# A quarter of the weights' low parts: one VectorE step in place of two GpSimd steps, with new instruction sequences

## The chip, the cores and the metric

The kernel runs on one core of a Trainium2 chip. The metric is device time in microseconds (us); before the change it is 901.27 us, the median of 3 runs (898.79 to 902.77). Five engines work side by side, each through its own list of instructions in order: TensorE (PE, with PEld for its weight loads), VectorE (DVE), ScalarE (ACT), GpSimd (POOL) and SyncE (SP), which issues the DMAs. An instruction that waits holds up everything behind it on its own engine.

## What is computed

Clustered attention over 4 batches, 8 heads, 768 positions of 64 elements, and on its output an MLP with a rational activation:

```python
mask = q_assign[:, :, :, None] == k_assign[:, :, None, :]      # nearest of 16 centroids, by cosine
scores = np.where(mask, scale * q @ k.T, -1e9)
x = softmax(scores) @ v                                        # -> (3072, 512)
h = x @ w_in                                                   # 512 -> 2048
P = a[0] + a[1] * h + a[2] * h * h + a[3] * h * h * h
Q = 1.0 + abs(b[0]) * abs(h) + abs(b[1]) * h * h
out = (P / (Q + 1e-6)) @ w_out                                 # 2048 -> 512
```

The results are wanted more exactly than one product of 16-bit numbers gives. So the kernel splits each matrix into a high part in f16 and a low part, the rest, also in f16, and adds three products: high by high, high by low, low by high.

## The kernel before

The program is made in two passes. The functions `weights`, `v_scale`, `g_scale`, `prep`, `attend`, `attend_keys` and `moe` only note down operations: engine, a cost in ns, what is read and written, which buffers are claimed. Each operation has a number, in the order in which it was noted. Then `Plan.order` emits them; the order on each engine is not planned in this kernel but given, as the lists of numbers in `ORDER` (lines 31 to 174). So a change in the number of operations renumbers what follows, and the lists must be written anew.

`weights(name, i, vt)` prepares one of 8 blocks of the MLP's weights, 4 of `w_in` ("wi") and 4 of `w_out` ("wo"), in the order wi0, wo0, wi1, wo1 and so on. A block has four chunks `c` of 128 partitions by 512 words. For each chunk:

- SP loads the raw 64-bit words (tile `rwi` or `rwo`).
- ACT takes the magnitude (line 672), and DVE makes an f32 number of it in three instructions: a shift (685), an or with the low word (690) and the sign (697). The tile is then `wwi` or `wwo`.

When all four are there, PE sums the squares (711), a power-of-two scale comes out of it, and for each pair of chunks `m`:

- ACT writes the high part into `win` or `wout`, 1024 columns at a time (749; in the trace all ACT work is on line 535, in the helper).
- For each of the two chunks POOL scales the f32 number in place (line 766) and subtracts the high part from it (line 773), which leaves the low part in f16.

The code has held another way for that last step since before: where `share("wlo", c)` is true, one DVE instruction does scale and subtract (lines 755 to 762). `share(name, i)` reads a fraction from `K`; `wlo` is not in `K`, so it is 0 and no chunk takes that way.

The blocks are spread over the first 200 us or so, between the work of batch 0. In that batch `attend_keys` works on four pairs of heads: `s` scores by PE (1391), the largest of each row by DVE out of PSUM (`top`, 1418), the scores turned round (`z`, 1470), the exponent by ACT (`at`), and the product with the values in f32 (1489, 1495). From about 180 us on `moe` (first product `ph`, 1622; second product `po`, 1733) runs on one batch, while `prep` and `attend` (scores 1261, 1277, 1323, values 1343) work on the next one. Since all engines serve both, the lists of `ORDER` set which goes first.

The names that the prediction uses: `win`, `wout` the split weights; `top`, `s`, `z`, `at`, `px`, `rs` of the attention; `ph`, `po`, `t`, `u` of the MLP; `tk`, `tq` the scaled keys and queries (1060, with a copy in 1080).

Of the kernel before, what the change touches and what calls it, by code (L numbers as in the profile page):

```python
# [27 lines left out]
K = {'ghd': 0.0, 'rvp': 0, 'look': 62.89, 'mulp': 0.4, 'sub': 0, 'xn': 14, 'NR': 8, 'sgp': 1, 'scp': 1, 'vsc': 0.75, 'sup0': 0, 'stk': 2, 'lop': 0, 'mgp': 0, 'rvn': 2, 'tq2': 2, 'at': 3, 'es': 4, 'vn': 3, 'ah': 5, 'rel': 0, 'twin': 1, 'pet': '_01', 'avs': 3, 'ksum': 1, 'fst': '_0', 'hpa': 1}  # L28
# [36 lines left out]
""",  # L65
    "DVE": """
# [310 lines left out]
def clustered_attention_moe_kernel(  # L377
# [167 lines left out]
    def dve(ns, fn, r, w, vt, claim=(), chain=None, lock=False, behind=()):  # L545
        return op("DVE", ns, fn, r, w, vt, claim, chain=chain, lock=lock, behind=behind)
# [1307 lines left out]
```

## Time and profile before

| | |
|---|---|
| time, median of 3 runs | 901.27 us (898.79 to 902.77) |
| the profiled execution | 901.28 us |
| its span (first to last instruction) | 899.1 us |
| PE, DVE, ACT, POOL busy | 851.8, 800.4, 772.2, 595.9 us |
| mean granted clock of TensorE | 0.994 |

Busy times are sums over the span; an engine may be busy and yet not be what the others wait for. In the timelines a bracket at a line's end tells how long the engine stood idle before that instruction and what ended the wait. The columns of a table of stretches are: the stretch, its length, the busy time of each engine in it with the number of its instructions, the granted clock, the share of the DMA engines and GB/s.

### The profile page before, as it was taken

Reading aid. Unit: us, or ns where it says so; the run is one execution under the profiler, and the core shown is the slowest. Engines: PE = TensorE matmul, PEld = TensorE weight load, DVE = VectorE, ACT = ScalarE, POOL = GpSimd, SP = SyncE. Lnnn points to the kernel's source line nnn. Section 1 sums busy time; section 2 is a strip of 40 time slices with the busy share of each in tenths; the row PEclk is TensorE's granted clock in tenths of the full one; section 3 lists DMA queues with packets and bytes.
Section 4 is the critical chain, followed back from the end, with each engine's and each line's share of the span. In section 5 each row is a group of like instructions: output and inputs, shape, how many; then the busy total and the mean of one; then the engine's idle time right before and its main releaser. Section 6 shows DMA issues by size and latency. Waiting matters only on the chain. (4 is left out here: it accounts for less than half of the span.)

```text
span 899.1 us, 20440 instructions
## 1 busy us (share of the span) xinstructions
PE 851.8 (95%) x7781; PEld 589.0 (66%) x7781; DVE 800.4 (89%) x1603; ACT 772.2 (86%) x1194; POOL 595.9 (66%) x623
## 2 busy tenths in 40 slices
PE   3799999898999999899999999999999999999997
PEld 2467676675767676566676666676667666667663
DVE  7998989689999999999999999999989989777775
ACT  7568787899999999998999999999998989767664
POOL 1354775599887978676888878788887866222221
PEclk9999999999999999999999999999999999999999
DMA  8488574658989688999799898888568855300000
GB/s 269 129 227 179 157 213 125 187 99 184 168 182 208 128 162 179 171 174 210 145 192 167 150 204 173 163 155 160 113 130 147 153 109 104 83 2 24 1 24 24
DMA packets 344802, 129.82 MB, mean 144 GB/s; under 512 B 322560, under 2 KB 338944, under 8 KB 344704
## 3 DMA queue, kind: packets, MB, share of 16 engines
q1 hardware_dynamic: 344704, 128.52, 67.4%
q8 instruction: 61, 1.00, 0.5%
q14 instruction: 37, 0.30, 0.1%
HBM read 41.98 MB, written 6.29 MB: 54 GB/s over the span
## 5 line engine op out<-in xcount | busy, mean ns | idle before, releaser
L1733 PE MATMUL po<-wout,u 128*128 128x512 f16 x1152 | 266.5, 379 | 0.1
L1622 PE MATMUL ph<-x,win 128*128 128x256 f16 x2304 | 264.6, 273 | 0.8 <-DVE t L1648 0.7
L1622 PEld LDWEIGHTS <-win 128*128 128x128 f16 x2304 | 225.2, 98 | 39.6 <-issue 1.1
L1662 POOL TENSOR_TENSOR s<-s,u 128x512 f32<-128x512 f32 x96 | 124.0, 1311 | 102.3 <-ACT s L535 54.9
L1733 PEld LDWEIGHTS <-u 128*128 128x128 f16 x1152 | 111.6, 98 | 120.1 <-issue 2.0
L1323 DVE SCALAR_TENSOR_TENSOR ah<-s,su,ah 128x768 f16<-128x768 f32 x144 | 143.2, 1012 | 13.1 <-ACT ah L535 11.5
L1277 DVE TENSOR_SCALAR_CACHE_REDUCE s<-s,cc 128x768 f32<-128x768 f32 x144 | 143.6, 1019 | 8.2 <-PE s L1261 7.1
L535 ACT ACTIVATE s<-s,nm 128x768 f32<-128x768 f32 x144 | 126.1, 877 | 12.1 <-DVE s L1277 10.0
L535 ACT ACTIVATE ah<-s,su 128x768 f16<-128x768 f32 x144 | 127.3, 904 | 5.3 <-ACT s L535 3.2
L1261 PE MATMUL s<-sk,sq 128*128 128x384 f16 x576 | 113.2, 329 | 6.3 <-DVE ah L1323 5.8
L1722 POOL TENSOR_TENSOR u<-s,u 128x512 f16<-128x512 f32 x72 | 83.5, 1169 | 50.5 <-DVE s L1715 26.8
L1685 POOL TENSOR_TENSOR s<-s,u 128x512 f32<-128x512 f32 x72 | 100.3, 1404 | 19.1 <-ACT u L535 18.7
L1261 PEld LDWEIGHTS <-sq 128*128 128x128 f16 x576 | 52.8, 98 | 49.9 <-DVE ah L1323 11.6
L1343 PE MATMUL px<-at,vhi 128*64 128x256 f16 x864 | 74.7, 275 | 2.5 <-DMA at<-ah 1.7
L1643 DVE TENSOR_TENSOR t<-ph,t 128x512 f32<-128x512 f32 x96 | 65.2, 683 | 8.1 <-ACT t L535 7.8
L535 ACT ACTIVATE u<-ph 128x512 f32<-128x512 f32 x96 | 57.3, 598 | 17.1 <-PE ph L1622 16.3
L1343 PE MATMUL px<-at,vlo 128*64 128x256 f16 x432 | 60.8, 273 | 0.0
L1715 DVE SCALAR_TENSOR_TENSOR s<-s,t 128x1024 f32<-128x1024 f32 (+1 forms) x49 | 60.2, 1228 | 0.5
L535 ACT ACTIVATE u<-t 128x1024 f16<-128x1024 f32 (+1 forms) x49 | 51.1, 1043 | 8.8 <-DVE s L1678 4.5
L1343 PEld LDWEIGHTS <-vhi 128*64 128x64 f16 x864 | 46.9, 110 | 17.0 <-issue 8.1
L535 ACT ACTIVATE t<-ph,gk 128x512 f32<-128x512 f32 x72 | 55.7, 778 | 0.0
L535 ACT ACTIVATE at<-z,cc 128x768 f32<-128x768 f32 x48 | 42.0, 897 | 15.7 <-PE z L1470 14.8
(222 smaller groups left out, 1541.6 us busy)
## 6 DMA issues: line engine op xcount, KB each, us to landing
rwi<-in_moe_w_in_dram SPq DMA_DIRECT2D x16, 512.0 KB, 4.8
rwo<-in_moe_w_out_dram SPq DMA_DIRECT2D x16, 512.0 KB, 4.6
rk<-in_k_dram SPq DMA_DIRECT2D x32, 192.0 KB, 3.2
rq<-in_q_dram SPq DMA_DIRECT2D x32, 192.0 KB, 3.3
rvm<-in_v_dram SPq DMA_DIRECT2D x16, 384.0 KB, 4.4
rv<-in_v_dram SPq DMA_DIRECT2D x16, 384.0 KB, 4.1
out_dram<-ob SPq DMA_DIRECT2D x11, 512.0 KB, 3.0
at<-ah SPq DMA_TRANSPOSE x144, 3.9
```

What stands on the lines that cost most here:

```text
L535: lambda: nc.scalar.activation(out=out(), in_=in_(), func=func, **{a: (x() if callable(x) else x) for a, x in kw.items()}),
L1261: nc.tensor.matmul(sc.ap[:, i, :SH], lhsT=st["q" + x].ap[:, j, t, :], rhs=st["k" + x].ap[:, j, ks, :].rearrange("p t c -> p (t c)"), start ...
L1277: lambda nm=nm, view=view: ts(out=view(), in0=view(), scalar1=cc.ap, scalar2=None, op0=ALU.mult, op1=ALU.min, accum_out=nm.ap),
L1323: lambda part=part, view=view, su=su: stt(out=part(1), in0=view(), scalar=su.ap, in1=part(0), op0=ALU.mult, op1=ALU.subtract),
L1343: nc.tensor.matmul(px.ap[j * D : (j + 1) * D, :], lhsT=vv.ap[:, j, kt, :], rhs=at[j].ap[:, p_, kt].rearrange("p t c -> p (t c)"), start=(i ...
L1622: nc.tensor.matmul(ph[i].ap[:, fi * TW : (fi + 1) * TW], lhsT=win[f // 4][:, wpart, c, f % 4 * P : (f % 4 + 1) * P], rhs=xs[c].ap[:, xpart ...
L1643: lambda i=i, th=th, ph=ph: tt(out=th[i].ap, in0=ph[i].ap, in1=th[i].ap, op=ALU.mult),
L1662: lambda i=i, sh=sh, uh=uh: nc.gpsimd.tensor_tensor(out=sh[i].ap, in0=sh[i].ap, in1=uh[i].ap, op=ALU.mult),
L1685: lambda i=i, sh=sh, uh=uh: nc.gpsimd.tensor_tensor(out=sh[i].ap, in0=sh[i].ap, in1=uh[i].ap, op=ALU.mult),
L1715: lambda tw=tw, sw=sw: stt(out=sw(), in0=sw(), scalar=2.0, in1=tw(), op0=ALU.subtract, op1=ALU.mult),
L1722: lambda i=i, sh=sh, gl=gl, g16=g16, e=(nc.vector if gld else nc.gpsimd): e.tensor_tensor(out=gl[i].ap, in0=sh[i].ap, in1=g16()[:, 0, i * ...
L1733: nc.tensor.matmul(po[ti].ap, lhsT=g16()[:, part, c0 : c0 + P], rhs=wout[f // 4][:, wpart, f % 4], start=(k == 0 and f == f_first), stop=( ...
```

## The change

`K` gets `'wlo': 0.25`. With it `share("wlo", c)` is true for c = 3 alone, so in each of the 8 blocks the fourth chunk's low part is made by one DVE instruction, and the two POOL instructions for it are gone. Each block has 35 operations in place of 36.

The lists in `ORDER` are written anew for all five engines, over the whole run. With the numbers brought back to the old ones, the longest run of operations that stands in the same relative order in both lists is 1094 of 1381 on DVE, 858 of 1001 on ACT, 662 of 789 on PE, 405 of 588 on POOL and 234 of 348 on SP. Most moves are by one to four places.

A further branch, `share("sgm", c)`, is added in the loop over the chunks, but `sgm` is not in `K`: it is never taken.

```diff
-K = {'ghd': 0.0, ..., 'hpa': 1}
+K = {'ghd': 0.0, ..., 'hpa': 1, 'wlo': 0.25}

 ORDER = {   (all five lists)
...
-            dve(
-                dc(512),
-                lambda w=w, word=word: stt(
-                    out=w.ap, in0=word(1), scalar=-2147483648, in1=w.ap, op0=ALU.bitwise_and, op1=ALU.bitwise_or
-                ),
-                [raw], [w], vt, [*hold, tok], lock=True,
-            )
+            if share("sgm", c):
+                act(
...
+            else:
+                dve(
+                    dc(512),
+                    lambda w=w, word=word: stt(
+                        out=w.ap, in0=word(1), scalar=-2147483648, in1=w.ap, op0=ALU.bitwise_and, op1=ALU.bitwise_or
+                    ),
+                    [raw], [w], vt, [*hold, tok], lock=True,
+                )
```

The step that is taken for c = 3, unchanged in the code:

```python
dve(
    dc(512, 1),
    lambda c=c, h=hl[d]: stt(
        out=h.ap[:, 1], in0=wf(c), scalar=sc(), in1=h.ap[:, 0], op0=ALU.mult, op1=ALU.subtract
    ),
    [ws[c], ws_], [hl[d]], vt, [wp[m], ptok[m]], lock=True,
)
```

## Rows read from the trace of the kernel before

**Rows 1.** The page's first part: busy time, share of the span, instructions.
```profile
PE 851.8 (95%) x7781; PEld 589.0 (66%) x7781; DVE 800.4 (89%) x1603; ACT 772.2 (86%) x1194; POOL 595.9 (66%) x623
```

**Rows 2.** Table of stretches, the run in three parts.
```profile
0.00:28.00 28.00, 12.54 (x136) 10.58 (x137) 21.25 (x73) 20.32 (x35) 4.39 (x21) 1.00 0.78 260
28.00:215.00 187.00, 168.91 (x1989) 123.21 (x1988) 166.14 (x352) 145.10 (x246) 122.46 (x154) 0.97 0.65 164
215.00:894.00 679.00, 670.30 (x5656) 455.20 (x5656) 612.40 (x1180) 606.09 (x915) 469.08 (x449) 1.00 0.69 134
```

**Rows 3.** Table of stretches, the part in which weights are prepared, by stage.
```profile
28.00:62.00 34.00, 26.82 (x262) 17.05 (x262) 33.80 (x62) 17.67 (x28) 18.14 (x24) 0.95 0.64 168
62.00:90.00 28.00, 27.95 (x361) 21.32 (x358) 24.23 (x59) 23.59 (x39) 12.34 (x18) 1.00 0.76 184
90.00:110.00 20.00, 19.10 (x221) 13.60 (x221) 19.70 (x36) 13.79 (x24) 14.22 (x16) 1.00 0.46 147
...
130.00:153.00 23.00, 21.25 (x214) 14.89 (x214) 22.75 (x47) 13.98 (x26) 13.51 (x20) 1.00 0.43 128
153.00:180.00 27.00, 23.54 (x344) 18.19 (x341) 18.12 (x44) 23.68 (x44) 16.91 (x26) 0.94 0.74 195
180.00:215.00 35.00, 30.25 (x312) 23.17 (x311) 31.33 (x69) 34.03 (x59) 31.82 (x35) 0.95 0.65 131
```

**Rows 4.** Lines 766 and 773: ns min/median/max, first and last start in us.
```profile
L766 POOL TENSOR_SCALAR wwi<-wwi,wis x16: 687/693/1911, 34.5 to 175.4; 128x512 f32<-128x512 f32 x16
...
L773 POOL TENSOR_TENSOR win<-wwi,win x16: 1148/1158/1866, 36.7 to 186.5; 128x512 f16<-128x512 f32 x16
```

**Rows 5.** DVE's timeline: start, duration, line, operation, tiles.
```profile
25.14 0.69 DVE L690 SCALAR_TENSOR_TENSOR wwi<-rwi,wwi 128x512 int32<-128x512 int32 x1
25.75 0.69 DVE L690 SCALAR_TENSOR_TENSOR wwo<-rwo,wwo 128x512 int32<-128x512 int32 x1
```

**Rows 6.** Groups on DVE, 28 to 215 us: busy us, mean ns, idle before.
```profile
L697 DVE SCALAR_TENSOR_TENSOR wwo<-rwo,wwo 128x512 int32<-128x512 int32 x15 | 12.1, 807 | 0.1
...
L1060 DVE SCALAR_TENSOR_TENSOR tq<-rq,qsc,tq 128x768 f16<-128x768 f32 x5 | 6.8, 1357 | 0.5 <-ACT tq L535 0.5
...
L1060 DVE SCALAR_TENSOR_TENSOR tk<-rk,ksc,tk 128x768 f16<-128x768 f32 x5 | 5.2, 1045 | 0.0
```

**Rows 7.** Timelines around 85 us: ACT's high part for wi1, and DVE.
```profile
84.26 1.14 ACT L535 ACTIVATE win<-wwi,wis 128x1024 f16<-128x1024 f32 x1
...
85.71 0.48 DVE L1540 SCALAR_TENSOR_TENSOR rs<-px,ev,rs 128x256 f32<-128x256 f32 x1 [0.60 <-ACT rs L535]
```

**Rows 8.** Timelines around 380 us, of DVE (two lines) and of PE.
```profile
379.95 0.35 DVE L1080 COPY tk<-tk 128x768 f16<-128x768 f16 x1
380.22 1.01 DVE L1323 SCALAR_TENSOR_TENSOR ah<-s,su,ah 128x768 f16<-128x768 f32 x1
...
381.29 0.82 PE L1261 MATMUL s<-sk,sq 128*128 128x384 f16 x4 [0.89 <-DVE ah L1323]
```

**Rows 9.** Timelines: POOL's last low part, and PE's first use of `wout`.
```profile
196.24 1.45 POOL L773 TENSOR_TENSOR wout<-wwo,wout 128x512 f16<-128x512 f32 x1
...
215.72 1.46 PE L1733 MATMUL po<-wout,u 128*128 128x512 f16 x6
```

**Rows 10.** PE's timeline, three waits between 158 and 207 us.
```profile
160.76 1.86 PE L1470 MATMUL z<-sq,sk 128*128 128x256 f16 x12 [2.44 <-ACT at L535]
...
204.75 0.71 PE L1532 MATMUL px<-rs,pick 128*128 128x128 f32 x4 [2.77 <-DVE rs L1524]
...
206.88 2.74 PE L1261 MATMUL s<-sk,sq 128*128 128x384 f16 x8 [1.30 <-DVE ah L1323]
```

**Rows 11.** ACT's timeline just before the first of these waits ends.
```profile
159.25 0.66 ACT L535 ACTIVATE wwo<-rwo 128x512 f32<-128x512 f32 x1 [1.80 <-DMA rwo<-in_moe_w_out_dram]
```

**Rows 12.** Table of stretches, two of 10 us with a lower granted clock.
```profile
160.00:170.00 10.00, 9.24 (x116) 7.40 (x115) 7.59 (x16) 9.93 (x18) 4.04 (x9) 0.83 0.88 256
200.00:210.00 10.00, 5.93 (x46) 3.19 (x35) 9.23 (x21) 9.94 (x18) 9.63 (x9) 0.83 0.94 198
```

More of the change, by code (lines that the diff above doesn't have):

```diff
@@ L25 @@
 M_BIG, M_MID, M_LOW = 2.0 ** 15, 2.0 ** 7, 2.0 ** -4
-K = {'ghd': 0.0, 'rvp': 0, 'look': 62.89, 'mulp': 0.4, 'sub': 0, 'xn': 14, 'NR': 8, 'sgp': 1, 'scp': 1, 'vsc': 0.75, 'sup0': 0, 'stk': 2, 'lop': 0, 'mgp': 0, 'rvn': 2, 'tq2': 2, 'at': 3, 'es': 4, 'vn': 3, 'ah': 5, 'rel': 0, 'twin': 1, 'pet': '_01', 'avs': 3, 'ksum': 1, 'fst': '_0', 'hpa': 1}
+K = {'ghd': 0.0, 'rvp': 0, 'look': 62.89, 'mulp': 0.4, 'sub': 0, 'xn': 14, 'NR': 8, 'sgp': 1, 'scp': 1, 'vsc': 0.75, 'sup0': 0, 'stk': 2, 'lop': 0, 'mgp': 0, 'rvn': 2, 'tq2': 2, 'at': 3, 'es': 4, 'vn': 3, 'ah': 5, 'rel': 0, 'twin': 1, 'pet': '_01', 'avs': 3, 'ksum': 1, 'fst': '_0', 'hpa': 1, 'wlo': 0.25}
 ORDER = {
     "ACT": """
[32 rows of a table removed]
[32 rows of a table added]
 """,
     "DVE": """
[44 rows of a table removed]
[44 rows of a table added]
 """,
     "PE": """
[25 rows of a table removed]
[25 rows of a table added]
 """,
     "POOL": """
[19 rows of a table removed]
[19 rows of a table added]
 """,
     "SP": """
[12 rows of a table removed]
[12 rows of a table added]
 """,
@@ L694, in weights @@
             )
-            dve(
-                dc(512),
-                lambda w=w, word=word: stt(
-                    out=w.ap, in0=word(1), scalar=-2147483648, in1=w.ap, op0=ALU.bitwise_and, op1=ALU.bitwise_or
-                ),
-                [raw], [w], vt, [*hold, tok], lock=True,
-            )
+            if share("sgm", c):
+                act(
+                    ac(512) + 65, lambda word=word: word(1).bitcast(F32), lambda word=word: word(1).bitcast(F32), AF.Sign, [raw], [raw],
+                    vt, [tok],
+                )
+                op(
+                    "POOL", 1400,
+                    lambda w=w, word=word: nc.gpsimd.tensor_tensor(
+                        out=w.ap.bitcast(F32), in0=w.ap.bitcast(F32), in1=word(1).bitcast(F32), op=ALU.mult
+                    ),
+                    [raw], [w], vt, [*hold, tok],
+                )
+            else:
[3 more added lines that the diff above has]
+                        out=w.ap, in0=word(1), scalar=-2147483648, in1=w.ap, op0=ALU.bitwise_and, op1=ALU.bitwise_or
+                    ),
+                    [raw], [w], vt, [*hold, tok], lock=True,
+                )
         gram = misc([P, P], F32, f"{name}g{i}")
```

264 rows, old and new, of the table ORDER are left out of this document.

## The prediction

> **What bounds the kernel now.** I read the page's first part, then tables of stretches, then timelines at the places where TensorE (PE) stands still. PE is busy for 851.8 of 899.1 us [rows 1], so the whole span holds 47 us in which it does nothing. The table in three parts says where: 15.5 us of them before 28 us (28 less 12.54), 18.1 between 28 and 215 us, 8.7 between 215 and 894 us, and the last 5 us, when the output leaves [rows 2]. The weights are prepared in the first two parts. After 215 us PE is 98.7% busy: what reaches that point late ends late by the same amount, and little can be won behind it except out of those 8.7 us.
>
> By stage, the part from 28 to 215 us has different limits [rows 3]. From 28 to 62 us VectorE (DVE) is busy 33.80 of 34 us and PE only 26.82: there DVE sets the pace. From 62 to 90 us PE is full (27.95 of 28) and DVE has 3.8 us to spare. From 90 to 110 and from 130 to 153 us both are nearly full (DVE 19.70 of 20 and 22.75 of 23, PE 19.10 and 21.25). From 153 to 180 us no engine is full: the stage is made of waits on each other. From 180 to 215 us ACT is the fullest, 34.03 of 35. GpSimd (POOL) is nowhere near full before the last stage. So the change takes work from an engine that is mostly not a limit and gives it to one that is a limit, alone or with PE, in three of these stages.
>
> **The change, part by part.** The profiled execution took 901.28 us, its span 899.1 and 2.2 around it; the median of the runs shown is 901.27, so a sum made against the profiled execution needs no correction.
>
> Removed: 8 times one scaling at 0.69 us and one subtraction at 1.16 us on POOL [rows 4], 14.8 us of work. That time itself is worth nothing at first: nobody waits for the low parts. The last of them is done at 197.7 us (196.24 and 1.45), and the first product with `wout` comes at 215.72 [rows 9].
>
> Added: 8 instructions on DVE, each of two inputs in SBUF and 512 columns. The trace shows no such instruction with this line. The nearest rows are of line 690, the same operation on 512 columns: 0.69 us for one, and two in a row start 0.61 us apart (25.14 and 25.75), so that is what one takes from DVE [rows 5]. To it comes what such an instruction loses when POOL works beside it: the 15 of line 697 on `wwo` have a mean of 0.807 us, 0.12 above the undisturbed 0.69 [rows 5, 6]. So one costs 0.73 us, and all eight 5.8 us of DVE.
>
> It also waits, like POOL's step before, for ACT's high part, and behind it on DVE stand row maxima (line 1418), for which PE's scores wait. The tightest place is the third: ACT writes that high part until 85.40 us (84.26 and 1.14), and the new list puts the instruction behind line 1540, which started at 85.71 [rows 7]. So the wait is over in time as long as both engines run as before, and I cost it at nothing; if ACT came 1 us later there, DVE would lose up to that 1 us, in a stage where it has 3.8 to spare.
>
> How much of this lies on the path? The new list of DVE in the diff tells next to which operations each one stands: the first in the stage from 28 to 62 us, the second and third between 62 and 90, the fourth between 90 and 110, the fifth and sixth between 130 and 153, the last two between 180 and 215. The first is on the path in full, 0.73. The second and third are covered by a full PE, the last two by DVE's 3.7 us of idle time in their stage [rows 3]; without that cover they would cost 0.73 each. The fourth to the sixth stand where DVE and PE are both nearly full; PE stands still for only 0.90 and 1.75 us there, so most of the delay is hidden, and I charge a third, 3 × 0.73 / 3 = 0.73. Together +1.5 us; the ends are 0 and 5.8.
>
> Given back: POOL's instructions disturb those of DVE less. Line 697 on `wwo` lost 15 × 0.12 = 1.8 us, line 1060 on `tq` 5 × (1.357 − 1.045) = 1.6 us against its twin on `tk` [rows 6], 3.4 us in all. A quarter of the 64 low-part instructions goes, so a quarter of that, −0.9 us. It can't be below nothing by much (the ends are 0 and −3.4).
>
> On the shared ports the rule of the Trainium skill ("SBUF — State Buffer", section "Who interferes with whom") is sharper than these means: a VectorE instruction with two SBUF inputs and a GpSimd instruction that reads SBUF exclude each other for the whole instruction, and who issues first wins. By that rule the new instruction pays nothing or up to a whole POOL instruction, not 0.12 us each time. In the rows only the mean over 15 is seen, and it speaks for few meetings; what the many would cost is the slower rival below.
>
> Moved: all five lists. Where an instruction of no urgency stood ahead of one that PE waits for, a new order can win that instruction's time. One such place can be read out of the diff: the copy of line 1080 at 379.95 us stands ahead of line 1323 at 380.22, for which PE waits 0.89 us [rows 8], and in the new list it comes later; that is worth 0.27 us, −0.3. I could not find one that loses for certain: on SP several transposes and loads go back behind others that wait for their data, but their users come much later. The rest of the moves I put at 0, between −8.7 us (all of PE's idle time after 215 us [rows 2]) and the same amount the other way, both unlikely.
>
> Sum: 1.5 − 0.9 − 0.3 = +0.3 on 901.28, that is **901.5 us**.
>
> **The rivals.** *Faster, by the stalls between 158 and 210 us.* PE waits there 2.44, 2.77 and 1.30 us [rows 10], and in two stretches of 10 us the granted clock falls to a mean of 0.83, a part of each at 1.2 in place of 2.4 GHz, after PE had stood still for some of the time [rows 12]; a loss of (1 − 0.83) × 10 = 1.7 us each at most. Together that is 6.5 + 3.4 = 9.9 us. These waits end with ACT and DVE, which have POOL's work in their chains; the last stage is the one in which POOL is busiest, 31.82 of 35 us [rows 3], and four of the removed instructions are near it. If half of the 9.9 us goes, and another 1 us of waits after 215 us with it, the time is 901.5 − 5.0 − 1.0 = 895.5. For it: the moves are many and go through all lists, and the stalls are few and large. Against it: the first wait ends only when ACT, held up for 1.80 us by a DMA of `rwo`, goes on [rows 11], and SP's list is the same around that DMA; DVE's work ahead of the other two is nearly the same set of instructions in both lists.
>
> *Slower, by the ports.* The new instruction stands on DVE near the other low parts of its block, which POOL still makes. If it meets a subtraction at its start, it waits up to the whole 1.16 us [rows 4], and everything behind it on DVE, row maxima and scores, waits too, and PE for those. The four that stand where DVE is nearly full would then cost 4 × (0.61 + 1.16) = 7.1 us in place of 1.5: 901.5 + 5.6 = 907.1. It decides from a mean wait of about 0.6 us for each of the four (4 × 1.21 − 1.5 = 3.4 us more, and with the relief gone 4.6). Against it: the mean loss of the same kind of instruction is 0.12 us [rows 5, 6].
>
> *Nothing but noise:* the change does what it says (`share` gives one chunk of four), but PE's full stages cover it and the moves cancel. That is 901.3, within the forecast's own range.
>
> **How the numbers follow.** A measurement of this kernel can tell about 0.5% from no change, 4.5 us. The forecast, with the third case in it, has 0.46 (897 to 905.8, from the ends of its terms); faster by the stalls or by the moves, 0.31; slower by the ports, or by a move that costs, 0.23. For 8 times in 10 the range must reach well into both rivals: from 894 us, the faster rival with 1.5 us more, to 908 us, the slower one with 1 us more.
>
> **What would show it.** Right: 16 instructions of lines 766 and 773 fewer in all, eight of line 758 on DVE with a mean near 0.8 us; DVE's busy time from 28 to 215 us up by 3 to 5 us; PE's start of the first `po` within 2 us of 215.7; PE's idle time after 215 us between 7 and 11 us. Wrong: the first `po` over 3 us earlier or later; the stretch from 200 to 210 us without its fall of the clock (the faster rival), or line 758 with a mean over 1.2 us (the slower one); or an idle time of PE after 215 us that has changed by more than 3 us, which no term of the sum foresees.

## The result: 0.6% slower, and the profile after

Beside each other the changed kernel took 905.68 us (median of 16 runs, 901.53 to 909.85), the kernel before 900.90 (median of 16, 898.04 to 903.17). The ratio is 1.0059, 95% interval 1.0046 to 1.0071: 5.3 us slower by the ratio, 4.1 to 6.4. The forecast was 901.5; the time lies in the stated range, on its slower side, nearer to the rival by the ports (907.1) than to the forecast. The profiled execution took 908.59 us, 2.9 above the median, and that will matter below.

From line 697 on the lines of the changed kernel stand 13 later (697 is 710, 1060 is 1073, 1733 is 1746); the new step is on line 771, POOL's pair on 779 and 786. First the page's first part, as in [rows 1]:

```profile
PE 855.2 (94%) x7781; PEld 591.5 (65%) x7781; DVE 805.3 (89%) x1611; ACT 775.1 (85%) x1194; POOL 585.2 (65%) x607
```

The table of stretches, as in [rows 2, 3, 12]:

```profile
0.00:28.00 28.00, 11.18 (x115) 9.56 (x116) 21.00 (x73) 19.46 (x34) 5.51 (x21) 1.00 0.82 258
28.00:215.00 187.00, 166.85 (x1964) 121.64 (x1963) 166.23 (x349) 141.34 (x236) 106.05 (x135) 0.98 0.63 160
215.00:901.60 686.60, 677.09 (x5707) 460.31 (x5705) 617.35 (x1190) 613.65 (x925) 473.69 (x452) 1.00 0.69 134
...
28.00:62.00 34.00, 26.66 (x257) 17.77 (x256) 30.98 (x57) 17.48 (x26) 11.39 (x16) 0.95 0.44 129
...
200.00:210.00 10.00, 7.45 (x94) 4.90 (x92) 9.32 (x21) 9.68 (x18) 9.74 (x9) 0.97 0.59 117
210.00:220.00 10.00, 8.14 (x50) 5.92 (x51) 9.74 (x21) 9.40 (x15) 6.65 (x7) 0.69 0.99 200
160.00:170.00 10.00, 7.33 (x114) 6.22 (x105) 8.23 (x18) 8.26 (x14) 5.19 (x6) 1.00 1.01 252
```

The change does what it says: 16 POOL instructions fewer, 8 more on DVE. DVE, which was busy 33.80 of 34 us from 28 to 62 us [rows 3], now has 3 us of idle time there, and PE no more work done: both wait. The fall of the clock near 205 us [rows 12] is not gone, it came later (0.69 from 210 to 220 us); the one near 165 us is gone in this execution (1.00). Behind 215 us PE stands still for 9.5 us (686.60 less 677.09), against 8.7 before [rows 2]. Of the 7.6 us by which the span of this execution is longer (906.7 against 899.1), 3.4 are not waits but busy time of PE: the same 7781 instructions take 855.2 us in place of 851.8. What made them longer was not traced.

Then the groups on DVE (busy us, mean ns, idle before): the new instruction over the whole run, and the lines of [rows 6] from 28 to 215 us:

```profile
L771 DVE SCALAR_TENSOR_TENSOR win<-wwi,wis,win 128x512 f16<-128x512 f32 x4 | 3.3, 837 | 0.0
L771 DVE SCALAR_TENSOR_TENSOR wout<-wwo,wos,wout 128x512 f16<-128x512 f32 x4 | 3.3, 835 | 0.0
...
L710 DVE SCALAR_TENSOR_TENSOR wwo<-rwo,wwo 128x512 int32<-128x512 int32 x16 | 12.5, 786 | 0.1
L1073 DVE SCALAR_TENSOR_TENSOR tq<-rq,qsc,tq 128x768 f16<-128x768 f32 x5 | 6.5, 1296 | 0.0
L1073 DVE SCALAR_TENSOR_TENSOR tk<-rk,ksc,tk 128x768 f16<-128x768 f32 x4 | 4.7, 1176 | 0.4 <-ACT tk L535 0.4
```

The timelines of POOL and PE: what answers to [rows 9], and the waits of PE that answer to [rows 8]:

```profile
201.24 1.44 POOL L786 TENSOR_TENSOR wout<-wwo,wout 128x512 f16<-128x512 f32 x1
221.76 1.46 PE L1746 MATMUL po<-wout,u 128*128 128x512 f16 x6
...
378.56 0.82 PE L1274 MATMUL s<-sk,sq 128*128 128x384 f16 x4 [0.61 <-DVE ah L1336]
382.81 0.82 PE L1274 MATMUL s<-sk,sq 128*128 128x384 f16 x4 [0.84 <-DVE ah L1336]
387.09 0.82 PE L1274 MATMUL s<-sk,sq 128*128 128x384 f16 x4 [0.86 <-DVE ah L1336]
```

The new instruction has a mean of 0.836 us. The first `po` comes at 221.76, 6.0 us later than before; most of the loss in this execution is there before the long stage begins.

To see where, I took every operation of PE in two traces and subtracted its start before from its start after: the lag. It is a number of two single executions. Medians by stretch, the time being that of the kernel before; the labels are those of the experiments below. From 84 to 96 and from 204 to 216 us the lag of several of these traces moves, and the median stands somewhere within the move:

```
us         after     e1     e5     e9    e10     e6    e11
 24- 30     1.78  -1.12   0.58   0.20  -1.40   0.29  -0.80
 60- 66     4.60  -0.79   0.37   0.21   2.57   2.74  -0.04
 84- 96     4.60  -0.79   0.37   3.84   3.72   7.23  -0.04
120-132     5.16   1.33   2.09   5.25   6.88  14.26   0.66
144-156     6.00   1.49   1.73   5.27   8.43  15.84   1.48
168-180     4.99  -0.12   0.12   5.34  11.61  19.60  -0.56
192-204     4.99  -0.12   0.11  10.37  11.61  23.52   0.07
204-216     6.07   0.48   0.12  10.91  12.32  24.35   1.39
240-300     5.57   0.71  -0.54  11.58  11.65  24.01   0.93
600-660     8.22   0.34  -0.09  13.33  16.33  29.54   3.39
840-900     7.85   0.25  -0.31  13.34  16.17  29.21   3.40
```

Each trace is of one execution, and not of the median one. The one of e1 took 901.05 us, where e1's median is 903.59: its lag ends at 0.25 us, so it holds next to nothing of the loss that e1's runs show. The one of e6 took 929.95, 5.4 above its median; those of e5, e9, e10 and e11 lie within 1.2 of theirs.

### The profile page after: what moved, and what is told of

It reads as the page before. It is cut to its first block, busy times and chain, and to the rows that moved or that the text cites. A ratio compares the mean times of both kernels' runs of the same rounds, so it can differ in the third digit from the quotient of the medians.

```text
span 906.7 us, 20418 instructions
## 1 busy us (share of the span) xinstructions
PE 855.2 (94%) x7781; PEld 591.5 (65%) x7781; DVE 805.3 (89%) x1611; ACT 775.1 (85%) x1194; POOL 585.2 (65%) x607
## 4 chain that ended last, share of the span: by engine, by line
PE 39%; DVE 6%; ACT 3%; issue 2%; DMA 1%; SPq 0%; DVEq 0%; ACTq 0%
PE po L1746 16%; PE ph L1635 15%; PE s L1274 4%; PE px L1356 3%; DVE s L1290 2%; DMA at<-ah 1%; DVE ah L1336 1%; ACT ah L535 1%; ACT s L535 1%; DVE t L1656 1%; ACT u L535 1%; DVE t L1661 1%; PE ptl L1160 0%; DVE s L1728 0%; ACT ob L535 0%
## 5 line engine op out<-in xcount | busy, mean ns | idle before, releaser
L535 ACT ACTIVATE s<-s,nm 128x768 f32<-128x768 f32 x144 | 126.5, 880 | 11.6 <-DVE s L1290 7.8
L1735 POOL TENSOR_TENSOR u<-s,u 128x512 f16<-128x512 f32 x72 | 84.2, 1182 | 47.4 <-DVE s L1728 24.8
L1661 DVE SCALAR_TENSOR_TENSOR t<-t,gk,ph 128x512 f32<-128x512 f32 x72 | 53.0, 742 | 0.9
```

What stands on the lines that cost most here:

```text
L535: lambda: nc.scalar.activation(out=out(), in_=in_(), func=func, **{a: (x() if callable(x) else x) for a, x in kw.items()}),
L1661: lambda i=i, th=th, ph=ph, col=col: stt(out=th[i].ap, in0=th[i].ap, scalar=col("a1")(), in1=ph[i].ap, op0=ALU.add, op1=ALU.mult),
L1735: lambda i=i, sh=sh, gl=gl, g16=g16, e=(nc.vector if gld else nc.gpsimd): e.tensor_tensor(out=gl[i].ap, in0=sh[i].ap, in1=g16()[:, 0, i * ...
```

## The experiments

All times are medians beside the kernel before on the same chip (900.1 to 901.2 us), with the 95% interval of the ratio. A loss in us is the ratio less 1 times that median.

### The step and the lists, one without the other

**e1, the step alone.** The new instruction, in the lists of before; it stands behind the same neighbours on DVE as in the new list.

```diff
-K = {..., 'hpa': 1}
+K = {..., 'hpa': 1, 'wlo': 0.25}
 ORDER = {   (the lists of before, renumbered, eight numbers put into DVE's)
```

> The step as in the changed kernel (eight low parts on DVE, 16 POOL instructions gone), but all five lists as before: only the removed numbers are taken out, and each new DVE instruction is put where the changed list has it relative to its neighbours. Theory A (the new lists made the loss, in the first 62 us): within 2 us of before, 899 to 903 us. Theory B (the step itself made it, by DVE time in the stages where DVE is full): 904 to 907 us, most of the loss of the changed kernel.

**e2, the lists alone.** The new lists, low parts on POOL as before; POOL's pair for the fourth chunk stands behind that for the third.

```diff
 K = {..., 'hpa': 1}
-ORDER = {   (the lists of before)
+ORDER = {   (the new lists, without the eight, sixteen numbers put into POOL's)
```

> The new lists, but the low parts made as before by POOL in two steps; in each block the two POOL instructions of the fourth chunk are put right behind those of the third, and the eight DVE instructions are taken out. Theory A: the loss stays, 904 to 907 us. Theory B: it goes, 899 to 902 us.

**e3 and e4, the lists in halves.** The step is in. e3 has the lists of before for the operations that started before 62 us and the new ones behind; e4 the other way round.

```diff
-ORDER = {   (new lists)
+ORDER = {   (e3: before's up to 62 us, new behind; e4: new up to 62 us, before's behind)
```

> The step, with the lists as before for all operations that started in the first 62 us of the profile of before, and the new lists from there on. Theory A: the 4.6 us by which PE is late at 62 us in the profile of the changed kernel are not lost, so 900 to 902 us, or a little above it if the 1 to 3 us that its profile shows later are of the new lists too. Theory B: the first new instruction stays where it was, so at most 1 us of the loss goes: 904 to 906 us.

> The other half: the step, with the new lists for the operations of the first 62 us, and the lists as before from there on. Theory A: the loss of the first 62 us is kept to the end, 904 to 906 us. Theory B: 904 to 906 us as well; so this one tells only whether what is lost early is kept (a time below 903 would mean that it is made up for later).

Measured: e1 903.59, ratio 1.0029 (1.0014 to 1.0045), a loss of 2.6 us; e2 907.45, 1.0070 (1.0050 to 1.0091), 6.3 us; e3 904.86, 1.0051 (1.0033 to 1.0070), 4.6 us; e4 904.86, 1.0045 (1.0028 to 1.0063), 4.1 us. Both theories were too simple. The step by itself costs, as B says, but only about half of the change's 5.3 us; the lists cost too, and not in their first 62 us alone: A wanted e3 back at 900 to 902. The two alone add up to 8.9 us, more than the change loses, so the new lists suit the kernel with the step better than the one without it (the place of POOL's extra pairs in e2 is in neither list, and can have a part in this).

### What of the step costs: VectorE's time, or its place

**e5.** As e1, but DVE's instruction is 16 columns wide.

```diff
-out=h.ap[:, 1], in0=wf(c), scalar=sc(), in1=h.ap[:, 0], op0=ALU.mult, op1=ALU.subtract
+out=h.ap[:, 1, :16], in0=wf(c)[:, :16], scalar=sc(), in1=h.ap[:, 0, :16], op0=ALU.mult, op1=ALU.subtract
...
+if b == 0 and hp == 0:     (once, near POOL's start)
+    for x in (*win, *wout):
+        nc.gpsimd.memset(x[:, 1, 3, 16:], 0.0)
```

> The step is in, in the lists of before (as in the run with the step alone), but VectorE's instruction works on 16 of its 512 columns only; the other 496 columns of the fourth chunk's low part are zeros, written once by GpSimd at 3.6 to 7 us, where it has nothing to do: so 16 GpSimd instructions are gone (14.8 us) and VectorE pays about 0.1 us in place of 0.73 for each of the eight. Theory C, the step's 2.6 us are VectorE's time on the path to the scores: they vanish here and only GpSimd's relief is left, 900 to 901.5 us. Theory D, the loss comes with the place of the instruction, whatever its length (it waits for ACT's high part or for GpSimd): 903 to 905, as for the step alone.

**e6.** The kernel before, and three DVE instructions more at each of the eight places.

```diff
-lambda c=c, h=hl[d]: stt(
-    out=h.ap[:, 1], in0=wf(c), scalar=sc(), in1=h.ap[:, 0], op0=ALU.mult, op1=ALU.subtract
-),
+lambda c=c, h=hl[d]: [stt(
+    out=junk, in0=ident[:, :64].unsqueeze(1).broadcast_to([P, 7, 64]),
+    scalar=sc(), in1=h.ap[:, 0, :448].rearrange("p (a b) -> p a b", b=64), op0=ALU.mult, op1=ALU.subtract
+) for _ in range(3)],
...
-else:
+if 1:     (POOL's two steps are kept)
```

> The kernel of before, GpSimd's sixteen instructions kept, and at each of the eight places of the step three VectorE instructions of two inputs and 448 columns that write to a scrap tile nobody reads: about 24 x 0.65 = 15.6 us more of VectorE. Theory C: the same share of VectorE's time is seen as for the step, 2.6 of 5.8 us or, with a relief of 0.9 us, 3.5 of 5.8; that is 7 to 9.5 us of 15.6, so 908 to 911, and TensorE falls behind by about 2 us at the first place (45 us) and at the fourth to the sixth (94 to 152 us), little at the others. If the places that a full TensorE covers aren't covered, 913 to 917. Theory D, a fixed price for each place: 903 to 906.

Measured: e5 900.4, ratio 1.0003 (0.9989 to 1.0018); e6 924.57, 1.0275 (1.0253 to 1.0296), a loss of 24.8 us. The instruction's grouped lines in e1, in e5 and in e6:

```profile
L788 DVE SCALAR_TENSOR_TENSOR wout<-wwo,wos,wout 128x512 f16<-128x512 f32 x4 | 3.2, 799 | 0.0
L788 DVE SCALAR_TENSOR_TENSOR win<-wwi,wis,win 128x512 f16<-128x512 f32 x4 | 3.0, 748 | 0.0
```

```profile
L788 DVE SCALAR_TENSOR_TENSOR wout<-wwo,wos,wout 128x16 f16<-128x16 f32 x4 | 1.1, 284 | 0.0
L788 DVE SCALAR_TENSOR_TENSOR win<-wwi,wis,win 128x16 f16<-128x16 f32 x4 | 0.9, 222 | 0.0
```

```profile
L790 DVE SCALAR_TENSOR_TENSOR junk<-ident,wos,wout 128x448 f16<-128x448 f32 x12 | 12.8, 1063 | 0.3
L790 DVE SCALAR_TENSOR_TENSOR junk<-ident,wis,win 128x448 f16<-128x448 f32 x12 | 9.6, 797 | 0.3
```

So 2.0 us of DVE's time cost nothing that can be told, 6.2 us cost 2.6, and 22.4 us cost 24.8. For the step it is the time that costs, not the place: theory D falls, with e5 at the time of before (e1 less e5 is 0.0026 of the ratio, give or take 0.0021, so only just clear). But C's "same share as for the step" falls too: e6 pays for its whole time, and more. Two things besides the amount differ between e6 and e1, and these runs don't separate them: e1 and e5 hold POOL's relief, and they have one instruction at each place, not three.

The lag of e1 is 1.49 us at 144 to 156 us and gone at 168. That isn't a wait of PE that swallowed it. Near 160 us PE stood still for 2.30 us in that trace (1.76 and 0.54), hardly less than the 2.44 before [rows 10]; but the fall of the clock that follows in the trace of before (0.94 from 153 to 180 us [rows 3], 0.83 from 160 to 170 [rows 12]) is missing:

```profile
153.00:180.00 27.00, 23.99 (x359) 18.67 (x356) 20.12 (x48) 25.24 (x48) 17.10 (x26) 1.00 0.87 206
```

Between 153 and 180 us the same instructions of PE took 1.2 us less busy time than before. Over its twelve runs, though, e1's granted clock has a mean of 0.9928, against 0.9942 in the 17 runs of before beside it, which is up to 1.2 us of its loss of 2.6 (1 less the clock, times the time).

### Is there cover

**e9 and e10.** As e6, with the three instructions at four places only. e9: the second, third, seventh and eighth, which the prediction held covered. e10: the first, fourth, fifth and sixth.

```diff
-for _ in range(3)]
+for _ in range(3 if 2 * i + (name == "wo") in (1, 2, 6, 7) else 0)]     # e10: (0, 3, 4, 5)
```

> The kernel of before with three extra VectorE instructions (as in the run with three at all eight places) at the second, third, seventh and eighth place only: the four that the prediction held covered, by a full TensorE from 62 to 90 us and by 3.7 us of VectorE's idle time from 180 to 215 us. Theory P, the cover is real, up to the idle time of VectorE in those stages (3.8 and 3.7 us): about 5.5 us of extra work in each of them, so 0 to 4 us more, 900 to 904.5 us. Theory Q, there is no such cover, since row maxima and scores queue behind the instruction in VectorE's fixed order, and TensorE has no other work in its own: nearly the whole 11 us are paid, 908 to 913.

> The same at the first, fourth, fifth and sixth place only: the four that the prediction put on the path, the first in full and the others by a third. Theory P: 2.5 us for the first and about 3 for the other three, 905 to 907. Theory Q: nearly the whole 11 us, 909 to 914. With all eight places it was 24.5 us more: if the two runs add up to much less, the loss grows faster than the work that is added.

Measured: e9 913.3, ratio 1.0135 (1.0115 to 1.0155), a loss of 12.2 us for 9.5 us of DVE's time (its two groups of line 790: 5.4 and 4.1); e10 918.0, 1.0191 (1.0165 to 1.0217), 17.2 us for 10.3. Theory Q, and e10 lies above its 914 too: rows of three, taken together, are not covered (at the second place alone the lag of e9 rises by 1.15 us for 2.05). The two losses add up to 29.4 us, more than the 24.8 of e6 with all eight; so, by the test set in e10's expectation, the loss does not grow faster than the work.

That both cost more than their DVE time goes with TensorE's clock. Its mean over the runs is 0.991 in e9, 0.988 in e10 and 0.987 in e6, against 0.994 to 0.995 in the runs of before beside them, which is at most 3.3, 6.5 and 7.0 us of the losses. PE's busy time for the same 7781 instructions, 851.8 us before, is 855.6, 856.5 and 862.6 in the three profiles. In e9 the clock fell in two stretches at or right behind the places; in both it was 1.00 before:

```profile
90.00:100.00 10.00, 7.52 (x40) 4.33 (x38) 8.69 (x15) 5.22 (x8) 9.10 (x11) 0.83 0.54 181
190.00:200.00 10.00, 8.16 (x58) 6.33 (x59) 9.50 (x22) 7.04 (x13) 8.13 (x11) 0.83 0.55 68
```

The timelines of e9 show how PE comes to wait. DVE first, then PE:

```profile
185.10 2.72 DVE L1113 COPY tq<-tq 128x768 f16<-128x768 f16 x1 [0.95 <-DMA sq<-tq]
...
187.86 2.11 DVE L790 SCALAR_TENSOR_TENSOR junk<-ident,wos,wout 128x448 f16<-128x448 f32 x3
189.89 1.02 DVE L1310 TENSOR_SCALAR_CACHE_REDUCE s<-s,cc 128x768 f32<-128x768 f32 x1
...
191.21 0.29 DVE L1557 SCALAR_TENSOR_TENSOR rs<-rs 128x128 f32<-128x128 f32 x1
...
191.55 0.71 PE L1565 MATMUL px<-rs,pick 128*128 128x128 f32 x4 [2.88 <-DVE rs L1557]
```

```profile
87.91 3.16 DVE L790 SCALAR_TENSOR_TENSOR junk<-ident,wis,win 128x448 f16<-128x448 f32 x3
90.99 0.34 DVE L1550 SCALAR_TENSOR_TENSOR rs<-px,eps,rs 128x128 f32<-128x128 f32 x1
91.25 1.81 DVE L1451 TENSOR_REDUCE top<-s 128x1 f32<-128x768 f32 x2
...
92.25 1.65 PE L1424 MATMUL s<-sk,sq 128*128 128x384 f16 x8 [2.03 <-DVE top L1451]
```

PE's `px` (1532 before) stands at the end of a chain on DVE into which the instructions were put; in the trace of before no wait of PE is listed between 178 and 193 us, here it is 2.88. Not all of that is theirs: the copy ahead of them took 2.72 us, and 0.83 before, with three of POOL's instructions beside it. Row maxima, which free the place for the next scores, queue behind the instructions in the same way at 88 us.

But the chain had room for a single one. In the trace of before DVE stood still in it for 1.17 us, waiting for scores:

```profile
180.86 1.02 DVE L1277 TENSOR_SCALAR_CACHE_REDUCE s<-s,cc 128x768 f32<-128x768 f32 x1 [1.17 <-PE s L1261]
```

And a single one is what the change puts there. Of the seven traces with the real step (the changed kernel, e1, e3, e4, e7, e8, e11) none has a lag of PE that differs by more than 0.01 us between 62 to 66 us and 90 to 94 us, across the second and third place; across the seventh and eighth, from 172 to 180 to 192 to 204 us, none by more than 0.01 but e11, where the seventh instruction took 1.74 us and PE lost 0.6. So at these four places the step cost PE nothing in all the other traces. Elsewhere it did. At the fourth the lag rises by 0.8 us in e1, e4 and e7, which have the lists of before there, and by 0.3 in e5; across the first, from 40 to 44 to 56 to 62 us, by 0.7 in e1 and e7 and 1.6 in e3, and by 0.2 in e5. (Under the new lists the lag rises by 0.8 at the fourth place in e2 too, without the step, so there it can't be told apart.)

### Where the lists lose

**e7, e8, e11.** All have the step. e7: lists of before up to 215 us, new ones behind. e11: new ones up to 215 us, those of before behind. e8: the changed kernel, with SP's and ACT's lists of before for the first 62 us.

```diff
-ORDER = {   (new lists)
+ORDER = {   (e7: before's up to 215 us, new behind; e11: new up to 215 us, before's behind;
+             e8: new, SP and ACT as before up to 62 us)
```

> The step is in; the lists of before up to 215 us, the new lists from there. Theory E, the new lists lose what they lose in the first 215 us, where the weights are formed: as the step alone, 903 to 904.5. Theory F, they lose as much in the long stage behind (TensorE of the changed kernel fell behind by another 1.9 us after 240 us): 905 to 906.5.

> The changed kernel, but SyncE's and ScalarE's lists of before for the first 62 us; VectorE's, TensorE's and GpSimd's are the new ones. In the changed kernel TensorE is 4.6 us behind at 62 to 96 us. Theory G, that comes from what SyncE and ScalarE put ahead (two loads ahead of the third load of w_in; a weight copy and two small steps ahead of a copy of the scores' input): TensorE is less than 2 us behind at 62 to 96 us, and the time is 903.5 to 905. Theory H, it comes from VectorE's and TensorE's own order: still 3.5 to 5 us behind there, and 905 to 906.5.

> The changed kernel with the lists of before from 215 us on (the counterpart of the run with the new lists from 215 us on). Theory F, the new lists lose about 2 us in the long stage behind 215 us: 903 to 904.5, and TensorE's lag stays at 6 us or falls after 360 us, where in the changed kernel it grew from 5.8 to 7.9. Theory E, they lose nothing there: 905 to 906.5, as the changed kernel.

Measured: e7 905.13, ratio 1.0051 (1.0035 to 1.0068); e8 905.17, 1.0056 (1.0039 to 1.0072); e11 905.05, 1.0052 (1.0033 to 1.0072). With e3 and e4 that makes five mixtures, and all lie between 1.0045 and 1.0056, between the step alone (1.0029) and the whole (1.0059). By its time e7 speaks for theory F and e11 for E, which exclude each other; e8's time speaks for H and its lag (1.65 us at 62 to 96 us) for G. So no half of the lists carries the loss alone, and it can't be placed with these runs.

Nor does one trace place it. The lag of the changed kernel, 4.6 us at 62 us, looks like the new lists' fault. But e11 has the same lists up to 215 us, and its lag at 62 us is −0.04. ACT's timeline of the two, the changed kernel first, and behind each the DMA issues of the first 34 us (count, size, median us from issue to landing):

```profile
9.89 0.67 ACT L535 ACTIVATE wwi<-rwi 128x512 f32<-128x512 f32 x1 [0.92 <-DMA rwi<-in_moe_w_in_dram]
11.16 0.66 ACT L535 ACTIVATE wwi<-rwi 128x512 f32<-128x512 f32 x1 [0.60 <-DMA rwi<-in_moe_w_in_dram]
...
24.02 0.67 ACT L535 ACTIVATE wwo<-rwo 128x512 f32<-128x512 f32 x1 [1.46 <-DMA rwo<-in_moe_w_out_dram]
```

```profile
rwi<-in_moe_w_in_dram SPq DMA_DIRECT2D x5, 512.0 KB, 6.8
rwo<-in_moe_w_out_dram SPq DMA_DIRECT2D x4, 512.0 KB, 7.2
```

```profile
8.16 0.64 ACT L552 ACTIVATE wwi<-rwi 128x512 f32<-128x512 f32 x1
9.45 0.68 ACT L552 ACTIVATE wwi<-rwi 128x512 f32<-128x512 f32 x1 [0.65 <-DMA rwi<-in_moe_w_in_dram]
...
21.98 0.67 ACT L552 ACTIVATE wwo<-rwo 128x512 f32<-128x512 f32 x1 [0.15 <-DMA rwo<-in_moe_w_out_dram]
```

```profile
rwi<-in_moe_w_in_dram SPq DMA_DIRECT2D x5, 512.0 KB, 5.0
rwo<-in_moe_w_out_dram SPq DMA_DIRECT2D x4, 512.0 KB, 5.6
```

Same order, same step at the same places, but the loads landed 1.6 to 1.8 us later in the one execution, and PE was 4.6 us later at 62 us. The profile of the changed kernel is of one such late execution.

That doesn't clear the new lists. Of the four traces that have them on all engines up to 62 us three are late there (the changed kernel 4.6 us, e2 4.5, e4 3.1) and one isn't (e11); of the five that have the lists of before there and no added rows of three at the first place (e1, e3, e5, e7, e9) none is later than 1.25. In e7 the loads of `rwi` landed as late as in the changed kernel (median 6.9 us), and PE was 1.25 us late. So it may be that the new lists pass a late load on to PE where the lists of before absorb most of it. Nine single traces point to it, and don't show it. And the first 62 us aren't the whole: e3 has the lists of before there and loses 4.6 us all the same.

### The relief

**e12.** The kernel before without POOL's two steps for the low parts, all 64 instructions.

```diff
-lambda c=c: nc.gpsimd.tensor_scalar(out=wf(c), ...)
+lambda: None
-lambda c=c, h=hl[d]: nc.gpsimd.tensor_tensor(out=h.ap[:, 1], ...)
+lambda: None
+for x in (*win, *wout): nc.gpsimd.memset(x[:, 1], 0.0)     # once, in POOL's first operation
```

> The kernel of before without any of GpSimd's 64 low-part instructions (59 us of GpSimd); nothing takes their place, the low parts are zeros that GpSimd writes once between 3.5 and 19 us, where it is idle. VectorE's list and work are those of before. Theory R, the relief is as the prediction sized it (line 697 on wwo and line 1060 on tq go back to their undisturbed 0.69 and 1.045 us, 3.4 us in all, and it reaches the end): 897 to 898.5 us, a quarter of it is the 0.9 us of the sum. Theory N, VectorE's time is given back, by the rows of the lines, but the time stays at 900 to 902: then the relief term was nothing, and the step's price is the whole of the loss with the step alone.

Measured: 909.07, ratio 1.0087 (1.0073 to 1.0100), a loss of 7.8 us that neither theory foresaw. It comes from my zeros. POOL's and DVE's timelines of e12, then of e5, where each of the memsets is a quarter as long:

```profile
3.53 7.05 POOL L1153 MEMSET win<- 128x2048 f16 x4
10.52 7.05 POOL L1153 MEMSET wout<- 128x2048 f16 x4
...
5.60 12.05 DVE L612 TENSOR_SCALAR cslot<-cslot,cr 128x64 f32<-128x64 f32 x2
```

```profile
3.54 1.88 POOL L1154 MEMSET win<- 128x496 f16 x4
...
5.59 0.82 DVE L611 TENSOR_SCALAR cslot<-cslot,cr 128x64 f32<-128x64 f32 x2
```

DVE's small instruction, 0.42 us for two in the trace of before, came through only when the last memset had ended (10.52 and 7.05 is 17.57; 5.60 and 12.05 is 17.65), and PE was 10.4 us late at 10 to 24 us. So the run can't settle what relief is worth in time. In the profiled execution, 3 us above the median, PE is still 11.6 us late at the end: nothing of the 10.4 came back. In the rows DVE did get time back (line 697 on `wwo`, line 728 there, has a mean of 686 ns over the run against 800 before). e5 is the better witness: all of the change's relief, 2.0 us of DVE's time, and 0.3 us of loss, −1.0 to 1.6.

## Why the prediction was right and wrong, point by point

**What bounds the kernel: right.** In the traces what was late when the long stage began stayed late, and PE's idle time behind 215 us is 9.5 us, within the 7 to 11 foretold.

**The price of the instruction: right in kind, a little small.** 0.73 us foretold; 0.836 in the changed kernel, 0.774 in e1. Six of the changed kernel's eight took 0.73 to 0.75, and two, with an instruction of POOL under way at their start, 1.12 and 1.14 (a third had one too and took 0.73): nothing or much, not 0.12 each time. The wait for ACT's high part, put at nothing, held: no idle time is listed before these instructions.

**How much of it lies on the path: the places were read rightly in the main, the price came out too low.** The four places called covered are covered in the traces, for one instruction of 0.7 us. The first, charged in full (0.73), cost 0.7 in two traces and more in a third. The fourth, charged a third (0.24), cost 0.8 where it can be read, its whole length: there the cover was not real. For the fifth and sixth the traces give no clear number. What e9 and e10 refute is cover for three in a row, 2 to 3 us at a place (12.2 us lost for 9.5; 17.2 for 10.3, where the rule of the prediction would give about 5). The list of an engine is fixed, and a chain that PE waits for has only so much room. With the relief the step was to cost 0.6 us, and it cost 2.6 (1.3 to 4.1). This is the first term of the sum that failed. The fourth place can be 0.6 of the missing 2 us, the relief, if it didn't come, 0.9, and the lower clock up to 1.2; how they share it is open, since the trace of e1 is of an execution that lost next to nothing.

**The relief, −0.9: not confirmed.** In the rows of the changed kernel line 697 on `wwo` and line 1060 on `tq` came down by 0.021 and 0.061 us [rows 6], 0.6 us in all, but `tk` on the same line went up from 1.045 to 1.176, 4 times, 0.5 us. What POOL no longer disturbs there it disturbs here.

**The moves, −0.3 and nothing else: wrong, the second term that failed.** The waits around 380 us are 0.61, 0.84 and 0.86 in place of 1.31 and 0.89 (the 1.31 ends with PE's instruction at 376.99 in the trace of before):

```profile
376.99 0.82 PE L1261 MATMUL s<-sk,sq 128*128 128x384 f16 x4 [1.31 <-DVE ah L1323]
```

That is 2.31 us against 2.20, so the moved copy brought nothing that can be seen. And the lists cost: the change less the step alone is 2.7 us (1.0059 less 1.0029, give or take 0.0020), or 6.3 us alone without the step. Where is open.

**The range: held by luck.** The sum foresaw +0.3 us and +5.3 was measured. The ends of the forecast itself, 897 to 905.8, let all eight instructions be paid in full and left out the ±8.7 us named for the moves. The range reached 908 only for the rival by the ports, whose mechanism did not come about; what came instead was a cost of the moves, named beside that rival only in its chance ("or by a move that costs") and put at 0 in the sum.

**The rivals.** *By the ports*: the time came near its 907.1, but not by its mechanism: it decides from a mean wait of 0.6 us, and the mean of the new line is 0.836, a wait of 0.1. (With the relief gone its text gives 4.6 us; its own 3.4 and 0.9 make 4.3.) *By the stalls*: one fall of the clock was missing in the profile after, the other came later and deeper, and the waits went on; no time was won. *Nothing but noise*: no, the interval leaves out 1.0000 by far, though the loss is barely more than the 0.5% that the text called distinguishable.

**The signs.** The first `po`, 6.0 us later, was the sign for "wrong", and rightly so in direction; its size belongs to one late execution. The stretch from 200 to 210 us had no fall of the clock to speak of (0.97), which was to be the sign for the faster rival; but the fall stood in the next stretch, so that sign told nothing. DVE's busy time from 28 to 215 us was to rise by 3 to 5 us and rose by 0.1 (166.23 against 166.14): it has three instructions fewer there in spite of the new ones, so work that had been done by 215 us slipped behind it. Over the whole run it rose by 4.9 (805.3 against 800.4).

## What to carry to other kernels

Idle time of an engine in a stage covers an instruction only as far as the chain that it is put into has room. Here one instruction of 0.7 us vanished at four places, and rows of three, taken together, were paid in full at the same ones. So a test three times as large tells that the cover ends, and not whether the small one was covered; for that, look at the lag of the bounding engine across the place, in several traces. Where the bounding engine is made to wait, its clock can fall too, so look at its busy time and the granted clock before giving a whole loss to the wait. And don't read a loss of a few us out of one trace: look first how far its execution lies from the median of its runs.

## What was not expected of the hardware

- A row of eight POOL memsets without a gap, 1.76 us each, kept a DVE instruction of 64 columns that started during the second waiting until the last had ended, 12.05 us; with memsets of 0.47 us the same one lost 0.4. The Trainium skill ("SBUF — State Buffer", section "Who interferes with whom") says, of a VectorE instruction in one of its two-port modes beside GpSimd, that who issues first gets the shared pair of ports for the whole instruction and the other is fully blocked. The rows agree with the block, but it lasted over seven instructions, not one; that the instruction was in such a mode, no run here shows. The copy of 2.72 us in e9 is of the same kind: it ended when a row of POOL's instructions did (186.45 and 1.15 is 187.60; 185.10 and 2.72 is 187.82).
- The three DVE instructions in a row took 0.67 to 0.69 us each when POOL left them alone, and up to 1.48 in the middle of its work, so that the 24 of e6 have means of 0.80 and 1.06 us by tile.
- Executions of the changed kernel scatter from 901.5 to 909.9 us, those of before from 898.0 to 903.2. In the pair of traces above the difference begins with loads in the first 25 us.
